# Second convolution as a six-stage pipeline in quarters of a chunk, with both parts of the spectral product summed on VectorE

## The chip, the cores and the metric

The kernel runs on one core of a Trainium2 chip. The metric is the device time of one execution in microseconds (us). Each kernel is run several times; the medians below come from runs in the fast state. A program on one core shows no die to compare with, so small differences are judged from several rounds and, inside the kernel, from the length of the changed stage in the profile.

In the profile the engines are PE (TensorE matmuls), PEld (TensorE weight loads), DVE (VectorE), ACT (ScalarE), POOL (GpSimd) and SP (SyncE, which issues the DMAs).

## The reference

A sequence of 2048 positions by 512 channels passes through four layers: convolution, attention, convolution, attention. The convolution, cut to what matters:

```python
def _A_ref(u, ...):                      # u: layernorm(x)
    K = ...                              # one real filter per channel, length L
    Kf = rfft(pad(K)); Uf = rfft(pad(u)) # along the sequence
    y = irfft(Uf * Kf)[:L]
    return y + u * Dskip
x = x + _A_ref(_layernorm(x), ...)       # first convolution
x = x + _B_ref(_layernorm(x), ...)       # attention in a sliding window
x = x + _A_ref(_layernorm(x), ...)       # second convolution: same filters
x = x + _B_ref(_layernorm(x), ...)
```

The kernel computes the transforms as matmuls. The filter spectra `Kt` are made during the first convolution and kept in memory, so the second one only loads them. It is the second convolution alone that the change rewrites.

## The kernel before

The 512 channels are four chunks of 128. Each chunk is worked in four quarters in the frequency part. The order in the second convolution is: forward transform of chunk dc+1, then products, inverse and final step of chunk dc.

```python
    def u_fft(self, dc, ln):
        dsl = slice(dc * DCH, (dc + 1) * DCH)
        U = self.one.tile([128, NJ, DCH], BF, name="U", tag="U")
        for j in range(NJ):                                   # 16 per chunk
            ln.norm(U[:, j, :], self.X[:, j, dsl], j)          # VectorE, 128 columns
        Z = self.s1(lambda j: U[:, j, :], DCH)                 # 32 matmuls, 4 copies by ScalarE
        xc = self.one.tile([128, 4, 2, 512], BF, name="xc", tag="xc", bufs=2)
        self.s2(Z, 4, [xc[:, c] for c in range(4)], "xc")      # per quarter: 8 transposes, zt on
        return xc                                              # VectorE, 4 matmuls, xc on ScalarE

    def finish(self, dc, xc, Kt, c0=0, c1=4):
        # ... (cut)
        def inverse(c, pa, pb):
            vp = self.pst([128, 2, 32, 2, 8])
            for g in range(4):
                sl = slice(g * 128, (g + 1) * 128)
                o = vp[:, g // 2, :, g % 2, :]
                nc.tensor.matmul(o, pa[:, 0, sl], IC[:, 0, :], start=True, stop=False)
                nc.tensor.matmul(o, pb[:, 1, sl], IC[:, 1, :], start=False, stop=False)
                nc.tensor.matmul(o, pb[:, 0, sl], IC[:, 2, :], start=False, stop=False)
                nc.tensor.matmul(o, pa[:, 1, sl], IC[:, 2, :], start=False, stop=True)
            # ... copy of vp to VT: first half by ScalarE, second half by VectorE
        pend = None
        for c in range(c0, c1 + 1):
            # ... (cut): pa and pb of this quarter
                nc.vector.tensor_tensor(pa[:], xc[:, c], Kt[:, c, 0:1, :].to_broadcast([128, 2, 512]), ALU.mult)
                nc.vector.tensor_tensor(pb[:], xc[:, c], Kt[:, c, 1:2, :].to_broadcast([128, 2, 512]), ALU.mult)
            # ... inverse of the quarter before
        # ... final: 32 + 4 matmuls a chunk, two copies to X by ScalarE

def a_layer(nc, tc, C, X, kt_dram, ln, ln_b):       # second convolution
        # ... (cut): pools (psA: 3 PSUM buffers), load of Kts, layernorm statistics
        xcs = {0: cv.u_fft(0, ln)}
        for dc in range(4):
            if dc < 3:
                xcs[dc + 1] = cv.u_fft(dc + 1, ln)
            cv.finish(dc, xcs.pop(dc), Kts[dc])
            if dc == 2:
                ln_b.gather(X, 0, 0, NJ)
        ln_b.gather(X, 1, 0, NJ)
        ln_b.finish(0, NJ)
```

The complex product is (xr + i xi)(Kr + i Ki). `pa` holds xr Kr and xi Kr, `pb` holds xr Ki and xi Ki. The sum xr Kr - xi Ki is not formed: the inverse lets TensorE add the parts in PSUM, which takes 16 matmuls of 256 columns a quarter. The order written here is not the order in which the engines run it: a scheduler in the framework orders the instructions of each engine.

Of the kernel before, what the change touches and what calls it, by code (L numbers as in the profile page):

```python
# [11 lines left out]
ALU = mybir.AluOpType  # L12
AX = mybir.AxisListType
F32 = mybir.dt.float32
BF = mybir.dt.bfloat16
# [4 lines left out]
D = 512  # L20
# [4 lines left out]
NJ = 16  # L25
# [3 lines left out]
DCH = 128  # L29
# [126 lines left out]
class Conv:  # L156
# [19 lines left out]
    def s1(self, rhs_j, n, drow=None):  # L176

        nc, F1 = self.nc, self.C["F1"]
        Z = self.z.tile([128, 2, 16, 128], BF, name="Z", tag="Z")
        for jq in range(NJ // 4):  # L180
            ps = self.pst([128, 2, 16, 32])
            for jj in range(4):
                j = jq * 4 + jj
                for r in range(2):
                    dk = drow is not None and j == 0 and r == 0
                    o = ps[:, r, 0:n // 8, jj * 8:(jj + 1) * 8]
                    nc.tensor.matmul(o, F1[:, j, r, :], rhs_j(j), start=True, stop=not dk)  # L187
                    if dk:
                        nc.tensor.matmul(o, self.C["onesr"][:], drow, start=False, stop=True)
            self.evac("z", Z[:, :, 0:n // 8, jq * 32:(jq + 1) * 32], ps[:, :, 0:n // 8, :])  # L190
        return Z

    def s2(self, Z, cs, dsts, what):

        nc, ident, C2 = self.nc, self.C["ident"], self.C["C2"]
        zts = {}

        def turn(i):
            pt = self.psT.tile([128, 2, 4, 128], BF, name="pt", tag="psT")
            for r in range(2):  # L200
                for g in range(4):
                    nc.tensor.transpose(pt[:, r, g, :], Z[:, r, i * 4 + g, :], ident[:])  # L202
            zt = self.w.tile([128, 2, 512], BF, name="zt", tag="zt")
            self.evac("zt_" + what, zt[:].rearrange("q r k -> q (r k)"), pt[:].rearrange("q r g k -> q (r g k)"))
            zts[i] = zt

        turn(0)
        for i in range(cs):
            if i + 1 < cs:
                turn(i + 1)  # L210
            zt = zts.pop(i)
            xp = self.pst([128, 2, 512])
            nc.tensor.matmul(xp[:, 0, :], C2[:, 0, :], zt[:, 0, :], start=True, stop=False)  # L213
            nc.tensor.matmul(xp[:, 0, :], C2[:, 2, :], zt[:, 1, :], start=False, stop=True)
            nc.tensor.matmul(xp[:, 1, :], C2[:, 1, :], zt[:, 0, :], start=True, stop=False)
            nc.tensor.matmul(xp[:, 1, :], C2[:, 0, :], zt[:, 1, :], start=False, stop=True)  # L216
            self.evac(what, dsts[i], xp[:])
# [329 lines left out]


def a_layer(nc, tc, C, X, kt_dram, ln, ln_b):
    with ExitStack() as es:  # L550
        kp = es.enter_context(tc.tile_pool(name="a_kt", bufs=4))
        psA = es.enter_context(tc.tile_pool(name="a_psA", bufs=3, space=PSUM))
        psT = es.enter_context(tc.tile_pool(name="a_psT", bufs=2, space=PSUM))
        Kts = []
        for dc in range(4):
            Kt = kp.tile([128, 4, 2, 512], BF, name="Kt", tag="Kt")
            nc.sync.dma_start(Kt[:], kt_dram[dc])
            Kts.append(Kt)
        cv = Conv(nc, tc, es, C, X, psA, psT, ("zt_xc", "vt1"), pbufs=3, vbufs=2)
        for j in range(0, NJ, 4):  # L560
            ln.gather(X, 0, j, j + 4)
        ln.finish(0, NJ)
        xcs = {0: cv.u_fft(0, ln)}
        for dc in range(4):
            if dc < 3:
                xcs[dc + 1] = cv.u_fft(dc + 1, ln)
            cv.finish(dc, xcs.pop(dc), Kts[dc])
            if dc == 2:
                ln_b.gather(X, 0, 0, NJ)
        ln_b.gather(X, 1, 0, NJ)  # L570
        ln_b.finish(0, NJ)
# [188 lines left out]
def kernel(  # L760
# [27 lines left out]
    Wt, Vp = load_b_weights(nc, tc, const2, B_wqkv, B_wo)  # L788
    b_layer(nc, tc, C, X, Wt, Vp, ln_b)
    a_layer(nc, tc, C, X, kt_dram, ln, ln_b)  # L790
    ov = out[0].rearrange("(p j) d -> p j d", j=NJ)
    b_layer(nc, tc, C, X, Wt, Vp, ln_b, lambda j0, j1: nc.sync.dma_start(ov[:, j0:j1, :], X[:, j0:j1, :]))
# [30 lines left out]
```

## Time and profile before

| | before |
|---|---|
| median of 4 runs | 663.84 us (660.38 to 664.5) |
| profiled run, span | 662.2 us |
| second convolution, from its first normalisation (418.33) to the first normalisation of the next layer (526.67) | 108.34 us |

Part 1 of the page of the kernel before gives busy time (share of the span) and number of instructions:

```profile
PE 467.0 (71%) x5880; PEld 306.2 (46%) x5913; DVE 516.4 (78%) x1001; ACT 325.2 (49%) x428; POOL 12.6 (2%) x49
```

These shares average over very different stages. The table of stretches for the second convolution (columns: stretch, its length, busy time of each engine with instruction count, granted TensorE clock, DMA share, GB/s), first for the whole stage, then for one inverse phase of it:

```profile
core 0: us, PE busy (x) PEld busy (x) DVE busy (x) ACT busy (x) POOL busy (x), PEclk, DMA share, GB/s
418.33:526.67 108.34, 81.13 (x716) 59.98 (x720) 67.06 (x181) 48.41 (x57) 0.00 (x0) 0.88 0.08 35
446.49:453.11 6.62, 5.84 (x51) 4.75 (x49) 6.62 (x11) 2.34 (x4) 0.00 (x0) 1.00 0.01 1
```

Over the stage no engine is full: PE 75%, DVE 62%, ACT 45%. In the inverse phase of the second line DVE is busy 6.62 of 6.62 us and PE 5.84. This stretch is VectorE's part of the phase. TensorE's own inverse matmuls start earlier, and from 444.59 to 451.57 us TensorE is busy 6.98 of 6.98 us: 64 matmuls 0.109 us apart, 1.75 us a quarter.

The view of waits for the same stage (who waited for whom, us in total, times, longest):

```profile
ACT VT L174 <- PE psA L244: 23.1, 16, 7.4
DVE zt L172 <- PE pt L202: 17.8, 10, 7.9
```

ScalarE waits 23.1 us for inverse matmuls and VectorE 17.8 us for transposes. The timeline of VectorE shows the phases (columns: start, duration, engine, line, operation, out<-in, shapes, count, and in brackets the idle time before and what ended it):

```profile
442.96 0.69 DVE L172 COPY zt<-pt 128x1024 bf16<-128x1024 bf16 x1 [1.40 <-PE pt L202]
446.49 0.69 DVE L257 TENSOR_TENSOR pb<-xc,Kt 128x1024 bf16<-128x1024 bf16 x1 [2.84 <-PE psA L244]
447.10 0.68 DVE L256 TENSOR_TENSOR pa<-xc,Kt 128x1024 bf16<-128x1024 bf16 x1
447.71 0.68 DVE L172 CAST VT<-psA 128x512 bf16<-128x512 f32 x1
448.31 0.68 DVE L257 TENSOR_TENSOR pb<-xc,Kt 128x1024 bf16<-128x1024 bf16 x1
...
453.11 0.68 DVE L172 CAST VT<-psA 128x512 bf16<-128x512 f32 x1
458.89 2.99 DVE L153 TENSOR_SCALAR U<-X,ln_rstd_a,ln_nb_a 128x128 bf16<-128x128 bf16 x13 [5.09 <-PE psA L187]
```

The first pb had to wait until an inverse matmul was done (2.84 us): the product tiles have three buffers, and the inverse matmuls read them. From 446.49 to 453.11 VectorE issues pb, pa, VT without a pause, 0.60 us from start to start. Then nothing for 5.09 us, until TensorE has freed the single U buffer. The next chunk's forward phase follows. The phases alternate with a period of some 24 us a chunk.

### The profile page before, as it was taken

Reading aid. Unit: us, or ns where it says so; the run is one execution under the profiler, and the core shown is the slowest. Engines: PE = TensorE matmul, PEld = TensorE weight load, DVE = VectorE, ACT = ScalarE, POOL = GpSimd, SP = SyncE. Lnnn points to the kernel's source line nnn. Section 1 sums busy time; section 2 is a strip of 40 time slices with the busy share of each in tenths; the row PEclk is TensorE's granted clock in tenths of the full one; section 3 lists DMA queues with packets and bytes.
Section 4 is the critical chain, followed back from the end, with each engine's and each line's share of the span. In section 5 each row is a group of like instructions: output and inputs, shape, how many; then the busy total and the mean of one; then the engine's idle time right before and its main releaser. Section 6 shows DMA issues by size and latency. Waiting matters only on the chain. (4 is left out here: it accounts for less than half of the span.)

```text
span 662.2 us, 13624 instructions
## 1 busy us (share of the span) xinstructions
PE 467.0 (71%) x5880; PEld 306.2 (46%) x5913; DVE 516.4 (78%) x1001; ACT 325.2 (49%) x428; POOL 12.6 (2%) x49
## 2 busy tenths in 40 slices
PE   1102837766767867679985899687986599876896
PEld 0001534554554555343334666455655453336763
DVE  5999899999999991368878997856538659778960
ACT  5990434655555646346672134564453265753133
POOL 0000000000000002000000000000000000000000
PEclk9999977998897889779997999779989799986999
DMA  9000100200200203200003000600000000030011
GB/s 303 24 0 1 34 16 18 96 8 29 97 12 24 97 19 112 96 0 1 1 17 94 2 1 2 253 1 1 1 1 1 0 1 1 1 109 2 2 65 64
DMA packets 14794, 26.70 MB, mean 40 GB/s; under 512 B 4753, under 2 KB 10258, under 8 KB 13582
## 3 DMA queue, kind: packets, MB, share of 16 engines
q1 hardware_dynamic: 12334, 24.65, 10.5%
q10 hardware_dynamic: 2400, 1.18, 0.7%
q8 instruction: 46, 0.75, 0.5%
q14 instruction: 14, 0.11, 0.1%
HBM read 13.80 MB, written 8.39 MB: 34 GB/s over the span
## 5 line engine op out<-in xcount | busy, mean ns | idle before, releaser
L613 PE MATMUL ps_qk<-xnT,wqk 128*128 128x512 bf16 x246 | 61.2, 380 | 1.6 <-ACT kT_4692 L615 0.3
L187 PE MATMUL psA<-U,sb_F_128 128*128 128x128 bf16 x256 | 24.1, 241 | 47.0 <-issue 38.5
L174 ACT CAST Z<-psA 128x1024 bf16<-128x1024 f32 (+1 forms) x52 | 46.4, 962 | 20.7 <-issue 17.8
L174 ACT CAST xc<-psA 128x1024 bf16<-128x1024 f32 x32 | 32.0, 1012 | 46.5 <-PE psA L216 39.9
L187 PEld LDWEIGHTS <-sb_F_128 128*128 128x128 bf16 x416 | 27.0, 104 | 57.6 <-issue 51.3
L202 PE MATMUL pt<-sb_ident,Z 128*128 128x128 bf16 x384 | 37.9, 265 | 19.1 <-ACT Z L174 19.1
L174 ACT CAST VT<-psA 128x512 bf16<-128x512 f32 x48 | 26.5, 587 | 43.3 <-PE psA L244 43.3
L202 PEld LDWEIGHTS <-Z 128*128 128x128 bf16 x384 | 32.5, 122 | 31.2 <-ACT Z L174 21.5
L731 ACT CAST oT<-po 128x1024 bf16<-128x1024 f32 x16 | 15.4, 1015 | 58.7 <-PE po L728 58.7
L241 PE MATMUL psA<-sb_IC,pa 128*128 128x256 bf16 x128 | 35.9, 280 | 7.9 <-DVE pa L256 7.8
L172 DVE COPY zt<-pt 128x1024 bf16<-128x1024 bf16 x32 | 21.8, 690 | 23.4 <-PE pt L202 23.2
L153 DVE TENSOR_SCALAR U<-X,ln_rstd_a,ln_nb_a 128x128 bf16<-128x128 bf16 x128 | 33.9, 313 | 7.2 <-PE psA L187 7.1
L242 PE MATMUL psA<-sb_IC,pb 128*128 128x256 bf16 x128 | 36.1, 282 | 1.6 <-DVE pb L257 1.3
L613 PEld LDWEIGHTS <-wqk 128*128 128x128 bf16 x256 | 22.8, 98 | 29.5 <-issue 8.2
L737 PE MATMUL ps_o<-wo_t,oT 128*128 128x512 bf16 x122 | 33.6, 379 | 3.9 <-ACT oT L731 3.1
L244 PE MATMUL psA<-sb_IC,pa 128*128 128x256 bf16 x128 | 36.1, 282 | 0.0
L243 PE MATMUL psA<-sb_IC,pb 128*128 128x256 bf16 x128 | 36.1, 282 | 0.0
L461 PE MATMUL psk<-Ytab,Xtab 128*32 128x64 bf16 x1024 | 23.4, 207 | 12.9 <-DVE Ytab L445 7.0
L464 PE MATMUL psk<-Y2tab,Xtab 128*32 128x48 bf16 x1024 | 22.6, 203 | 13.3 <-issue 11.4
L655 PE MATMUL Lp<-prod,sb_bones 128*32 128x512 bf16 x256 | 24.7, 392 | 10.3 <-DVE prod L650 7.5
L213 PE MATMUL psA<-zt,sb_C_120 128*128 128x512 bf16 x48 | 22.7, 473 | 11.2 <-DVE zt L172 6.0
L140 DVE BATCH_NORM_STATS2 ln_st_b<-X 128x6 f32<-128x384 bf16 (+1 forms) x64 | 21.3, 413 | 11.4 <-ACT X L272 11.4
(402 smaller groups left out, 1211.1 us busy)
## 6 DMA issues: line engine op xcount, KB each, us to landing
Kt<-kt_scratch SPq DMA_DIRECT2D x4, 1024.0 KB, 7.0
Vp<-V SPq DMA_DIRECT2D x2, 1568.0 KB, 9.2
kt_scratch<-Kt SPq DMA_DIRECT2D x3, 1024.0 KB, 3.8
X<-in_A_u_dram SPq DMA_DIRECT2D x4, 512.0 KB, 5.5
k_scratch<-KTq SPq DMA_DIRECT2D x8, 256.0 KB, 2.4
KT<-k_scratch SPq DMA_DIRECT2D x8, 256.0 KB, 2.7
out_dram<-X SPq DMA_DIRECT2D x4, 512.0 KB, 2.6
sb_F_128<-c_F SPq DMA_DIRECT2D x1, 1024.0 KB, 5.9
```

The costliest lines, as they stand in the source:

```text
L153: self.nc.vector.tensor_scalar(dst, src, self.rstd[:, j:j + 1], self.nb[:, j:j + 1], ALU.mult, ALU.add)
L174: self.nc.scalar.copy(dst, src)
L187: nc.tensor.matmul(o, F1[:, j, r, :], rhs_j(j), start=True, stop=not dk)
L202: nc.tensor.transpose(pt[:, r, g, :], Z[:, r, i * 4 + g, :], ident[:])
L241: nc.tensor.matmul(o, pa[:, 0, sl], IC[:, 0, :], start=True, stop=False)
L242: nc.tensor.matmul(o, pb[:, 1, sl], IC[:, 1, :], start=False, stop=False)
L243: nc.tensor.matmul(o, pb[:, 0, sl], IC[:, 2, :], start=False, stop=False)
L244: nc.tensor.matmul(o, pa[:, 1, sl], IC[:, 2, :], start=False, stop=True)
L461: nc.tensor.matmul(psk[32 * g:32 * g + 32, ds, :], xs, Y[:, m // 2, h, :, t], start=(m == 0), stop=False, skip_group_check=True)
L613: nc.tensor.matmul(ps[:], wqk[:, ct, f0:f0 + 128], xnT[:, ct, s0:s0 + 512], start=(ct == 0), stop=(ct == 3))
L655: nc.tensor.matmul(Lp[r0:r0 + 32, w // 4, :], bones[:, w % 4, :], pr[:, f2, hb * 512:(hb + 1) * 512], start=(w % 4 == 0), stop=(w % 4 == 3 ...
L737: nc.tensor.matmul(ps[:], oT[:, ft, j * 128:(j + 1) * 128], wo_t[:, ft, :], start=(ft == 0), stop=False)
```

## The change

The intent is to keep all engines at work on different quarters at once. The stages of 16 quarters are issued with fixed lags, so that in one step the loop handles the forward matmuls of quarter k, the transposes of k-5, the second transform of k-6, the product of k-7, the inverse of k-8 and the final step of k-13. At the same time VectorE forms the complex sum `Y`, so the inverse needs 8 matmuls a quarter, not 16. The normalisation becomes 16 instructions of 512 columns ahead of the pipeline.

```diff
 def a_layer(nc, tc, C, X, kt_dram, ln, ln_b):
     with ExitStack() as es:
+        # ... pools: U whole, Z 3 buffers, xc 4, VT 2, work tiles 3
         psA = es.enter_context(tc.tile_pool(name="a_psA", bufs=3, space=PSUM))
         psT = es.enter_context(tc.tile_pool(name="a_psT", bufs=2, space=PSUM))
+        def s1(k):      # ... 8 matmuls, Z on ScalarE
+        def turn(k):    # ... 8 transposes, zt on VectorE
+        def s2(k):      # ... 4 matmuls, xc on ScalarE
+        def product(k):
+            # ...
+            nc.vector.tensor_tensor(pa[:], x[:], Kt[dc][:, c, 0:1, :].to_broadcast([128, 2, 512]), ALU.mult)
+            nc.vector.tensor_tensor(pb[:], x[:], Kt[dc][:, c, 1:2, :].to_broadcast([128, 2, 512]), ALU.mult)
+            nc.vector.tensor_tensor(Y[k][:, 0, :], pa[:, 0, :], pb[:, 1, :], ALU.subtract)
+            nc.vector.tensor_tensor(Y[k][:, 1, :], pa[:, 1, :], pb[:, 0, :], ALU.add)
+        def inverse(k):
+            # ...
+            for g in range(4):
+                nc.tensor.matmul(o, y[:, 0, sl], IC[:, 0, :], start=True, stop=False)
+                nc.tensor.matmul(o, y[:, 1, sl], IC[:, 2, :], start=False, stop=True)
+            # ... VT: half gh == 0 by ScalarE, half gh == 1 by VectorE, as before
+        def final(k):   # ... 1 + 8 matmuls, one copy to X by ScalarE
         # ... statistics, as before
-        xcs = {0: cv.u_fft(0, ln)}
-        for dc in range(4):
-            # ... (cut)
+        for j in range(NJ):
+            ln.norm(U[:, j, :], X[:, j, :], j)
+        for k in range(16 + 14):
+            for fn, lag in ((final, 13), (inverse, 8), (product, 7), (s2, 6), (turn, 5), (s1, 0)):
+                if 0 <= k - lag < 16:
+                    fn(k - lag)
+            if k == 13 + 11:
                 ln_b.gather(X, 0, 0, NJ)
         ln_b.gather(X, 1, 0, NJ)
         ln_b.finish(0, NJ)
```

More of the change, by code (lines that the diff above doesn't have):

```diff
@@ L550, in a_layer @@
     with ExitStack() as es:
+        big = es.enter_context(tc.tile_pool(name="a_big", bufs=1))
         kp = es.enter_context(tc.tile_pool(name="a_kt", bufs=4))
+        zp = es.enter_context(tc.tile_pool(name="a_z", bufs=3))
+        cp = es.enter_context(tc.tile_pool(name="a_xc", bufs=4))
+        vpool = es.enter_context(tc.tile_pool(name="a_vt", bufs=2))
+        wk = es.enter_context(tc.tile_pool(name="a_wk", bufs=3))
         psA = es.enter_context(tc.tile_pool(name="a_psA", bufs=3, space=PSUM))
@@ L553, in a_layer @@
         psT = es.enter_context(tc.tile_pool(name="a_psT", bufs=2, space=PSUM))
-        Kts = []
+        ident, C2, IC, F1, F1T = C["ident"], C["C2"], C["IC"], C["F1"], C["F1T"]
+        U = big.tile([128, NJ, D], BF, name="U")
+        Kt = []
         for dc in range(4):
-            Kt = kp.tile([128, 4, 2, 512], BF, name="Kt", tag="Kt")
-            nc.sync.dma_start(Kt[:], kt_dram[dc])
-            Kts.append(Kt)
-        cv = Conv(nc, tc, es, C, X, psA, psT, ("zt_xc", "vt1"), pbufs=3, vbufs=2)
+            t = kp.tile([128, 4, 2, 512], BF, name="Kt", tag="Kt")
+            nc.sync.dma_start(t[:], kt_dram[dc])
+            Kt.append(t)
@@ new lines, in a_layer @@
+        Z, zt, xc, Y, VT = {}, {}, {}, {}, {}
+        def s1(k):
+            dc, q = k // 4, k % 4
+            if q == 0:
+                Z[dc] = zp.tile([128, 2, 16, 128], BF, name="Z", tag="Z")
+            ps = psA.tile([128, 2, 16, 32], F32, name="ps_s1", tag="psA")
+            for jj in range(4):
+                j = q * 4 + jj
+                for r in range(2):
+                    nc.tensor.matmul(ps[:, r, :, jj * 8:(jj + 1) * 8], F1[:, j, r, :],
+                                     U[:, j, dc * DCH:(dc + 1) * DCH], start=True, stop=True)
+            nc.scalar.copy(Z[dc][:, :, :, q * 32:(q + 1) * 32], ps[:])
@@ new lines, in turn @@
+        def turn(k):
+            dc, c = k // 4, k % 4
+            pt = psT.tile([128, 2, 4, 128], BF, name="pt", tag="psT")
+            for r in range(2):
+                for g in range(4):
+                    nc.tensor.transpose(pt[:, r, g, :], Z[dc][:, r, c * 4 + g, :], ident[:])
+            zt[k] = wk.tile([128, 2, 512], BF, name="zt", tag="zt")
+            nc.vector.tensor_copy(zt[k][:].rearrange("q r k -> q (r k)"), pt[:].rearrange("q r g k -> q (r g k)"))
+        def s2(k):
+            z = zt.pop(k)
+            xp = psA.tile([128, 2, 512], F32, name="xp", tag="psA")
+            nc.tensor.matmul(xp[:, 0, :], C2[:, 0, :], z[:, 0, :], start=True, stop=False)
+            nc.tensor.matmul(xp[:, 0, :], C2[:, 2, :], z[:, 1, :], start=False, stop=True)
+            nc.tensor.matmul(xp[:, 1, :], C2[:, 1, :], z[:, 0, :], start=True, stop=False)
+            nc.tensor.matmul(xp[:, 1, :], C2[:, 0, :], z[:, 1, :], start=False, stop=True)
+            xc[k] = cp.tile([128, 2, 512], BF, name="xc", tag="xc")
+            nc.scalar.copy(xc[k][:], xp[:])
@@ new lines, in product @@
+        def product(k):
+            dc, c = k // 4, k % 4
+            x = xc.pop(k)
+            pa = wk.tile([128, 2, 512], BF, name="pa", tag="pa")
+            pb = wk.tile([128, 2, 512], BF, name="pb", tag="pb")
+            Y[k] = wk.tile([128, 2, 512], BF, name="Y", tag="Y")
+            nc.vector.tensor_tensor(pa[:], x[:], Kt[dc][:, c, 0:1, :].to_broadcast([128, 2, 512]), ALU.mult)
+            nc.vector.tensor_tensor(pb[:], x[:], Kt[dc][:, c, 1:2, :].to_broadcast([128, 2, 512]), ALU.mult)
+            nc.vector.tensor_tensor(Y[k][:, 0, :], pa[:, 0, :], pb[:, 1, :], ALU.subtract)
+            nc.vector.tensor_tensor(Y[k][:, 1, :], pa[:, 1, :], pb[:, 0, :], ALU.add)
@@ new lines, in inverse @@
+        def inverse(k):
+            dc, c = k // 4, k % 4
+            if c == 0:
+                VT[dc] = vpool.tile([128, 2, NJ, DCH], BF, name="VT", tag="VT")
+            y = Y.pop(k)
+            vp = psA.tile([128, 2, 32, 2, 8], F32, name="vp", tag="psA")
+            for g in range(4):
+                sl = slice(g * 128, (g + 1) * 128)
+                o = vp[:, g // 2, :, g % 2, :]
+                nc.tensor.matmul(o, y[:, 0, sl], IC[:, 0, :], start=True, stop=False)
+                nc.tensor.matmul(o, y[:, 1, sl], IC[:, 2, :], start=False, stop=True)
+            for gh in range(2):
+                x0 = c * 32 + gh * 16
+                dst = VT[dc][:, :, :, x0:x0 + 16].rearrange("k r j x -> k (r j) x")
+                src = vp[:, gh, :, :, :].rearrange("k rj g e -> k rj (g e)")
+                if gh == 0:
+                    nc.scalar.copy(dst, src)
+                else:
+                    nc.vector.tensor_copy(dst, src)
@@ new lines, in final @@
+        def final(k):
+            dc, q = k // 4, k % 4
+            dsl = slice(dc * DCH, (dc + 1) * DCH)
+            ps = psA.tile([128, 4, DCH], F32, name="ps_y", tag="psA")
+            j0 = q * 4
+            nc.tensor.matmul(ps[:], ident[:], X[:, j0:j0 + 4, dsl], start=True, stop=False, skip_group_check=True)
+            for jj in range(4):
+                for r in range(2):
+                    nc.tensor.matmul(ps[:, jj, :], F1T[:, j0 + jj, r, :], VT[dc][:, r, j0 + jj, :],
+                                     start=False, stop=(jj == 3 and r == 1), skip_group_check=True)
+            nc.scalar.copy(X[:, j0:j0 + 4, dsl], ps[:])
@@ L562, in a_layer @@
         ln.finish(0, NJ)
-        xcs = {0: cv.u_fft(0, ln)}
-        for dc in range(4):
-            if dc < 3:
-                xcs[dc + 1] = cv.u_fft(dc + 1, ln)
-            cv.finish(dc, xcs.pop(dc), Kts[dc])
-            if dc == 2:
+        for j in range(NJ):
[5 more added lines that the diff above has]
+            if k == 13 + 11:
                 ln_b.gather(X, 0, 0, NJ)
```

## The prediction

> **What bounds the kernel now.** The change touches only the second convolution. In the timeline it runs from the end of the statistics before it (418.3 us) to the first normalisation of the layer after it (526.7 us): 108.4 of 662.2 us. Within 425 to 526.2 us the table of stretches shows PE busy 76.5, DVE 60.4, ACT 44.7 of 101 us: nothing is full. The timeline shows why: four chunks go through phases in turn, each bound by another engine. Forward: copies of Z (ACT, 0.94 us pitch), then transposes, zt, matmuls, xc (DVE waits 17.8 us for transposes in the view of waits). Inverse: PE alone, 16 matmuls, 1.75 us a quarter, while ACT waits 23.1 us.
>
> **What changes, per quarter (16 of them), by pitches in the timeline.**
> - PE: inverse from 16 to 8 matmuls, 1.73 to 0.87 us at full clock. With forward 0.45, transposes 0.45, s2 0.86, final 0.67: 3.3 us.
> - DVE: adds a subtract and an add of 128x512 bf16. pa (128x1024) has 0.60 us pitch; half of it plus fixed cost gives an estimate of 0.33 each, and 0.1 for waits on its own products. The Trainium skill, "VectorE: DVE Perf Modes", section Mode 2×_1P, says packed 16-bit operands give two results a cycle; the 0.60 us agrees. With zt, pa, pb, VT at 0.60 each: 3.1 to 3.2 us.
> - ACT: Z 0.94, xc 0.97, VT 0.55, X 0.55: 3.0 us, nearly unchanged.
> - DVE normalisation: 64 instructions of 128 columns (0.23 each, 15 us) become 16 of 512 (0.37 each, 6 us), all ahead of the pipeline. This pays for most of the 10.6 us of adds.
>
> So DVE's work stays at 66 to 70 us and becomes, with PE, the limit. The gain comes from overlap and 14 us less PE work.
>
> **On the critical path.** Fill: norm until 424.3, last Z copy of chunk 0 about 425.5, first Y about 431. Then 15 quarters. The engines are balanced at 3.0 to 3.3 us and coupled: three PSUM buffers serve four tiles a quarter, and the final matmuls wait for the DVE copy of VT, which waits for the ACT copy. I estimate 3.6 us a quarter: last Y about 485. Drain: the scheduled DVE order puts the statistics of chunks 0 to 2 (16 x 0.47) after the last products, so about 13 us (7.5 + 0.6 + 3.2 + 1.3 + 0.9) lie between the last Y and the first normalisation: 498. The stage falls from 108 to about 80 us, saving 27 to 28. The other layers keep their times.
>
> **Clock.** "TensorE: Matmul & The Clock Gate", Part 1, says the array runs at half rate after an idle window. The trace agrees: s2 matmuls come 0.43 us apart near 426 and 487, 0.215 elsewhere. A pipeline leaves no such gaps except at its start, so I expect at least the present clock of 0.89.
>
> **Prediction: 637 us** (8 in 10: 627 to 648). Faster by over 2%: 0.94; within 2%: 0.05; slower: 0.01.
>
> **Right if** the stage takes 75 to 85 us; DVE and PE are busy 80% or more in its middle; successive pa come 3.3 to 3.9 us apart; Y subtract and add take 0.35 to 0.45 us; after the last VT copy DVE runs statistics back to back for some 10 us. **Wrong if** a quarter takes over 4.2 us, through the chain inverse, VT on ACT, VT on DVE, Y in one in-order queue, or late PSUM buffers, or half-clock spells; or if the layer after runs at another clock.

## The result and the profile after

| | before | after |
|---|---|---|
| median of 4 runs | 663.84 us | 630.23 us (627.81 to 631.95) |
| profiled run, span | 662.2 us | 630.0 us |
| second convolution | 108.34 us | 73.55 us (420.89 to 494.44) |

The ratio is 0.9501, with a 95% interval from 0.9449 to 0.9553. A ratio is the mean time of one kernel's fast runs over that of the other's of the same rounds, so it is not quite the ratio of the medians quoted. The stage became 34.8 us shorter and the span 32.2 us: the part ahead of the stage, whose code is the same, took 2.6 us more in this profile. Its end lies between 416.4 and 420.9 us in all profiles, in no order that follows the edits. So lengths of the stage are the sharper measure below. From the end of the stage to the end of the span it is 135.6 us after and 135.5 before.

Part 1 of the page of the kernel after:

```profile
PE 449.9 (71%) x5748; PEld 293.6 (47%) x5785; DVE 517.8 (82%) x985; ACT 326.2 (52%) x436; POOL 12.6 (2%) x49
```

VectorE's 517.8 us are the 516.4 of before within 0.3%, while TensorE has lost 17 us. The table of stretches, for the stage and for three parts of its middle (from the first pa to the last one; columns as in the table before):

```profile
420.89:494.44 73.55, 59.14 (x584) 43.75 (x592) 67.85 (x164) 49.30 (x65) 0.00 (x0) 0.92 0.12 50
432.46:450.30 17.84, 15.91 (x170) 11.73 (x171) 17.84 (x36) 14.62 (x18) 0.00 (x0) 1.00 0.01 1
450.30:463.28 12.98, 12.75 (x138) 9.96 (x138) 12.83 (x25) 11.66 (x16) 0.00 (x0) 1.00 0.01 3
463.28:478.42 15.14, 14.58 (x136) 10.27 (x137) 15.04 (x30) 10.95 (x16) 0.00 (x0) 1.00 0.00 1
```

VectorE is busy 99% of the middle (17.84 of 17.84, 12.83 of 12.98, 15.04 of 15.14 us), TensorE 89 to 98%, at a granted clock of 1.00. The view of waits answers to that of before:

```profile
ACT VT L627 <- PE vp L621: 6.3, 12, 0.9
...
DVE zt L588 <- PE pt L586: 3.4, 1, 3.4
```

ScalarE's wait for inverse matmuls fell from 23.1 to 6.3 us, and VectorE's wait for transposes from 17.8 to 3.4 us, all of it one wait in the start. VectorE's timeline, one early quarter and the start of a late one:

```profile
444.16 0.68 DVE L606 TENSOR_TENSOR pa<-xc,Kt 128x1024 bf16<-128x1024 bf16 x1
444.76 0.68 DVE L607 TENSOR_TENSOR pb<-xc,Kt 128x1024 bf16<-128x1024 bf16 x1
445.36 0.69 DVE L588 COPY zt<-pt 128x1024 bf16<-128x1024 bf16 x1
445.96 0.68 DVE L629 CAST VT<-vp 128x512 bf16<-128x512 f32 x1
446.56 0.42 DVE L608 TENSOR_TENSOR Y<-pa,pb 128x512 bf16<-128x512 bf16 x1
446.89 0.42 DVE L609 TENSOR_TENSOR Y<-pa,pb 128x512 bf16<-128x512 bf16 x1
447.23 0.69 DVE L606 TENSOR_TENSOR pa<-xc,Kt 128x1024 bf16<-128x1024 bf16 x1
...
460.06 0.68 DVE L606 TENSOR_TENSOR pa<-xc,Kt 128x1024 bf16<-128x1024 bf16 x1
460.66 0.68 DVE L607 TENSOR_TENSOR pb<-xc,Kt 128x1024 bf16<-128x1024 bf16 x1
461.38 0.42 DVE L608 TENSOR_TENSOR Y<-pa,pb 128x512 bf16<-128x512 bf16 x1
```

From pa to pa it is 3.07 us, and this is the plain sum of the starts: pa, pb, zt, VT at 0.60 each and Y twice at 0.33. No bracket: the view shows no wait of VectorE for another engine here. In the late quarter the subtract follows pb directly and starts 0.72 us after it, not 0.60: it needs pb's result, and no other instruction fills the 0.12 us. That gives 3.2 us a quarter. Two quarters took longer without a bracket, 3.15 us from 450.30 and 3.41 us from 453.45. In the second VectorE started VT and the next pa 0.07 and 0.13 us late; this pa followed the end of its xc copy on ScalarE by 0.04 us. The inputs come close before their use throughout: each xc copy ended 0.03 to 0.76 us before the pa that reads it. The end of the stage:

```profile
481.02 0.42 DVE L609 TENSOR_TENSOR Y<-pa,pb 128x512 bf16<-128x512 bf16 x1
481.36 1.93 DVE L140 BATCH_NORM_STATS2 ln_st_b<-X 128x6 f32<-128x384 bf16 x4
483.20 0.68 DVE L629 CAST VT<-vp 128x512 bf16<-128x512 f32 x1
483.81 8.24 DVE L140 BATCH_NORM_STATS2 ln_st_b<-X 128x6 f32<-128x384 bf16 x27
491.96 1.27 DVE L145 BATCH_NORM_AGGREGATE ln_mv_b<-ln_st_b 128x2 f32<-128x12 f32 x16
...
494.44 1.71 DVE L153 TENSOR_SCALAR xn<-X,ln_rstd_b,ln_nb_b 128x512 bf16<-128x512 bf16 x5
```

After the last add (481.02 + 0.42) VectorE works almost without pause for 13.0 us: 31 statistics and one VT copy, the aggregation, then small steps to the first normalisation of the next layer.

### The profile page after: what moved, and what is told of

Its sections match the earlier page's. It is cut to its first block, busy times and chain, and to the rows that moved or that the text cites. A ratio compares the mean times of both kernels' runs of the same rounds, so it can differ in the third digit from the quotient of the medians.

```text
span 630.0 us, 13342 instructions
## 1 busy us (share of the span) xinstructions
PE 449.9 (71%) x5748; PEld 293.6 (47%) x5785; DVE 517.8 (82%) x985; ACT 326.2 (52%) x436; POOL 12.6 (2%) x49
## 4 chain that ended last, share of the span: by engine, by line
PE 29%; DVE 23%; issue 7%; ACT 5%; DMA 1%; POOL 0%; ACTq 0%; POOLq 0%; DVEq 0%
PE ps_qk L697 8%; PE ps_v L707 4%; PE ps_o L821 4%; PE po L812 2%; DVE ln_st_b L140 2%; PE Lp L739 2%; DVE pa L606 1%; DVE pb L607 1%; DVE VT L629 1%; DVE zt L588 1%; DVE prod L734 1%; PE ps_o L823 1%; DVE xn L153 1%; DMA wo_t<-in_B_wo_dram 1%; ACT oT L815 1%
## 5 line engine op out<-in xcount | busy, mean ns | idle before, releaser
L187 PE MATMUL psA<-U,sb_F_128 128*128 128x128 bf16 x128 | 13.6, 249 | 41.8 <-issue 38.5
L174 ACT CAST Z<-psA 128x1024 bf16<-128x1024 f32 (+1 forms) x36 | 31.3, 928 | 18.4 <-issue 17.5
L202 PE MATMUL pt<-sb_ident,Z 128*128 128x128 bf16 x256 | 28.5, 287 | 11.8 <-ACT Z L174 11.8
L174 ACT CAST xc<-psA 128x1024 bf16<-128x1024 f32 x16 | 15.9, 1012 | 27.3 <-PE psA L216 27.3
L461 PEld LDWEIGHTS <-Xtab 128*32 128x32 bf16 x1024 | 20.7, 105 | 18.5 <-issue 17.6
L445 DVE TENSOR_TENSOR Ytab<-Ytab,MA 128x2048 bf16<-128x2048 bf16 x24 | 29.2, 1219 | 0.1
L447 DVE TENSOR_TENSOR Y2tab<-Ytab,MB 128x2048 bf16<-128x2048 bf16 x24 | 29.2, 1218 | 0.0
L707 PE MATMUL ps_v<-wv,xnT 128*128 128x512 bf16 x126 | 28.2, 379 | 0.1
L140 DVE BATCH_NORM_STATS2 ln_st_a<-X 128x6 f32<-128x512 bf16 x32 | 21.0, 686 | 7.1 <-ACT X L824 5.3
L824 ACT CAST X<-ps_o 128x512 bf16<-128x512 f32 x32 | 18.3, 586 | 16.0 <-PE ps_o L823 16.0
```

What stands on the lines that cost most here:

```text
L140: self.nc.vector.bn_stats(self.st[:, j, part, :], X[:, j, a:b])
L174: self.nc.scalar.copy(dst, src)
L187: nc.tensor.matmul(o, F1[:, j, r, :], rhs_j(j), start=True, stop=not dk)
L202: nc.tensor.transpose(pt[:, r, g, :], Z[:, r, i * 4 + g, :], ident[:])
L445: nc.vector.tensor_tensor(Y[:, :, :, q * EYB:(q + 1) * EYB, :].rearrange("n c h e t -> n (c h) e t"), src, self.mult(self.MA, lev, hc, EYB ...
L447: nc.vector.tensor_tensor(Y2[:, :, :, (q - 1) * EYB:q * EYB, :].rearrange("n c h e t -> n (c h) e t"), src, self.mult(self.MB, lev, hc, EY ...
```

## The experiments

The two marked kernels leave out part of the product, so their result is not the convolution. The check calls every run correct, these two as well; it therefore doesn't show that the sum of this layer is right. "Stage" is the time from the first normalisation of the second convolution to the first one of the next layer, read in the timeline of the profiled run; "pace" is the distance of successive pa.

| run | what | median us | ratio to before | stage us |
|---|---|---|---|---|
| e0_after_again | the changed kernel | 630.01 | 0.9494 | 73.54 |
| e1_pipe_only | pipeline, no sum, 16 inverse matmuls | 634.88 | 0.958 | 79.52 |
| e2_sum_only | old order, sum, 8 inverse matmuls | 652.85 | 0.984 | 95.93 |
| e9_old_no_sum | old order, 8 inverse matmuls, no sum (wrong result) | 648.49 | 0.9778 | 93.13 |
| e3_sum_twice | changed, sum done twice | 640.00 | 0.9649 | 83.78 |
| e4_no_sum | changed, no sum (wrong result) | 624.23 | 0.9411 | 68.15 |
| e5_norm_chunks | changed, normalisation by chunks | 633.72 | 0.9552 | 78.50 |
| e8_psum2 | changed, two PSUM buffers | 635.89 | 0.958 | 78.83 |
| e6_vt_late_act | changed, late VT on ScalarE | 625.68 | 0.9435 | 70.53 |
| e7_best | e6 plus two further moves | 626.31 | 0.9445 | 70.79 |

e1 to e4 share one chip and one set of runs of the kernel before (median 662.37), e0 and e5 to e7 another (663.91), e8 and e9 a third (663.26). e0, e5, e6 and e7 had five rounds, the others three.

The theory to test: the pipeline turns a chain of phases into one stage paced by its fullest engine, VectorE, at the sum of its instruction starts. The rivals: the gain is the saved TensorE work; or the pace is set by coupling, the loop from the inverse through the two VT copies, or the PSUM buffers, and VectorE only looks full.

### The changed kernel again

No edit. 

> The changed kernel itself, as the reference on this chip: 0.950 of the kernel before, 628 to 632 us; the stage 73.5 us again.

It measured as expected: 630.01 us and a stage of 73.54 us, 0.01 us from the first profile.

### The pipeline without the sum

```diff
-            nc.vector.tensor_tensor(Y[k][:, 0, :], pa[:, 0, :], pb[:, 1, :], ALU.subtract)
-            nc.vector.tensor_tensor(Y[k][:, 1, :], pa[:, 1, :], pb[:, 0, :], ALU.add)
+            Y[k] = (pa, pb)
 # and in inverse(k), the four matmuls of before:
-                nc.tensor.matmul(o, y[:, 0, sl], IC[:, 0, :], start=True, stop=False)
-                nc.tensor.matmul(o, y[:, 1, sl], IC[:, 2, :], start=False, stop=True)
+                nc.tensor.matmul(o, pa[:, 0, sl], IC[:, 0, :], start=True, stop=False)
+                nc.tensor.matmul(o, pb[:, 1, sl], IC[:, 1, :], start=False, stop=False)
+                nc.tensor.matmul(o, pb[:, 0, sl], IC[:, 2, :], start=False, stop=False)
+                nc.tensor.matmul(o, pa[:, 1, sl], IC[:, 2, :], start=False, stop=True)
```

> The pipeline without the sum on VectorE: products pa and pb go to the inverse unsummed, 16 matmuls a quarter again. Theory (the pipeline brings most of the gain and whichever engine has the most work per quarter sets the pace): VectorE needs about 2.45 us a quarter, TensorE about 3.5 (no final matmuls yet), 4.2 (all parts) and 3.7 (no forward part any more), so TensorE sets a pace of about 3.7 us against the 3.1 us of the changed kernel; the stage takes 80 to 86 us against 73.6, the whole 637 to 643 us, with TensorE busy over 95% and VectorE about 65% in the middle. Rival (the saved inverse matmuls bring the gain): 650 us or more.

It measured 634.88 us and a stage of 79.52 us, 0.5 us below the expected range; the whole was 2 us below its range. The pace was 3.50, 4.17 and 3.72 us in the three parts, which are the sums of TensorE's work. The table of stretches of this run, four quarters with all parts and then four without a forward part:

```profile
448.54:465.20 16.66, 16.55 (x180) 13.57 (x180) 10.50 (x17) 11.97 (x16) 0.00 (x0) 1.00 0.00 1
465.20:480.08 14.88, 14.77 (x148) 11.80 (x149) 10.50 (x18) 8.73 (x12) 0.00 (x0) 1.00 0.01 2
```

TensorE is busy 16.55 of 16.66 us and VectorE 10.50. The limit changed engines, as the theory said. The pipeline without the sum brings 28.8 of the 34.8 us of the stage. This run still holds everything but the sum: the lags, the added buffers and the normalisation in 16 instructions. A rival stays untested: no run gave the old order the added buffers, though its normalisation waited 6.2 us in all for the single U buffer, so what the lags bring by themselves is not shown.

### The sum in the old order

```diff
+        self.summed = summed        # True only for the second convolution
 # in inverse:
+                if self.summed:
+                    nc.tensor.matmul(o, pa[:, 0, sl], IC[:, 0, :], start=True, stop=False)
+                    nc.tensor.matmul(o, pa[:, 1, sl], IC[:, 2, :], start=False, stop=True)
+                    continue
 # after pa and pb:
+                if self.summed:
+                    Y = self.p.tile([128, 2, 512], BF, name="Y", tag="Y")
+                    nc.vector.tensor_tensor(Y[:, 0, :], pa[:, 0, :], pb[:, 1, :], ALU.subtract)
+                    nc.vector.tensor_tensor(Y[:, 1, :], pa[:, 1, :], pb[:, 0, :], ALU.add)
+                    pa = Y
```

> The old order of phases with the sum on VectorE in the second convolution only. Theory: the inverse phase, which TensorE bounded at 1.75 us a quarter, becomes a VectorE phase of about 2.5 us (pa, pb, VT at 0.6 and the two halves of Y at 0.33), so taking 14 us of work off TensorE gains nothing; 660 to 675 us. Rival (TensorE work was the limit of the old kernel, so halving the inverse pays by itself): 648 to 653 us.

My theory missed: 652.85 us, within the rival's range, and a stage 12.4 us shorter. In the timeline of VectorE in this run the products stand elsewhere:

```profile
462.01 0.69 DVE L173 COPY zt<-pt 128x1024 bf16<-128x1024 bf16 x1 [1.29 <-PE pt L203]
462.62 0.68 DVE L261 TENSOR_TENSOR pa<-xc,Kt 128x1024 bf16<-128x1024 bf16 x1
463.21 0.68 DVE L262 TENSOR_TENSOR pb<-xc,Kt 128x1024 bf16<-128x1024 bf16 x1
464.04 0.69 DVE L173 COPY zt<-pt 128x1024 bf16<-128x1024 bf16 x1
464.65 0.68 DVE L261 TENSOR_TENSOR pa<-xc,Kt 128x1024 bf16<-128x1024 bf16 x1
465.24 0.68 DVE L262 TENSOR_TENSOR pb<-xc,Kt 128x1024 bf16<-128x1024 bf16 x1
466.73 0.42 DVE L265 TENSOR_TENSOR Y<-pa,pb 128x512 bf16<-128x512 bf16 x1 [0.80 <-PE psA L244]
```

The products of two quarters sit between the zt copies of the next chunk's forward phase. In the kernel before, 13 of the 16 pairs of products came once an inverse phase had begun, since its matmuls held the product buffers (VectorE waited for them 2.84, 2.77 and 2.77 us). Here only the adds read pa and pb, so these are free again early; what waits for an inverse matmul now is the subtract (0.80 us), whose Y tile has three buffers of its own. So the idle time of the forward phase took part of the work. I had counted VectorE's work of the inverse phase as bound to that phase.

### The old order with the short inverse and no sum

This is the edit of the run before without the two lines that form Y; the inverse reads pa alone, so the result is wrong.

> Wrong result on purpose: the old order of phases, eight inverse matmuls, no subtract and add. It splits the 10 us that the sum alone gained in the old order. Theory, formed after that run: TensorE was on the path of the inverse phase, so halving it pays nearly its full 14 us, and the adds cost some 2 to 5 us of the 10.6 they take, since VectorE waits elsewhere: 646 to 650 us. Rival: the adds cost nothing there: 652 us. Second rival: they cost their full 10.6 us: 641 us.

It measured 648.49 us, within the expected range, and a stage of 93.13 us. So in the old order the shorter inverse gave 15.2 us of the stage, and the adds took back 2.8 us of it, though VectorE was busy 10.0 us longer with them (77.59 against 67.57 us): most of that fell into idle time. The timeline of VectorE also shows which products moved:

```profile
460.64 0.69 DVE L262 TENSOR_TENSOR pb<-xc,Kt 128x1024 bf16<-128x1024 bf16 x1
461.31 0.69 DVE L173 COPY zt<-pt 128x1024 bf16<-128x1024 bf16 x1
461.92 0.68 DVE L262 TENSOR_TENSOR pb<-xc,Kt 128x1024 bf16<-128x1024 bf16 x1
...
464.01 0.69 DVE L261 TENSOR_TENSOR pa<-xc,Kt 128x1024 bf16<-128x1024 bf16 x1
```

Only pb, which nothing reads in this run, comes between the zt copies; pa, which the inverse reads, still comes after the first inverse matmul (462.94 us), though VectorE stood idle for 0.62 us before the third pb, which came at 463.22 us. With the inverse equally short in both runs, this points to the buffers, and not to the shorter inverse, as what let the products move. One thing stays open: the 15.2 us mix two effects, less TensorE work (128 matmuls at 0.109 us are 14 us) and products that get a buffer earlier. No run held the order fixed.

### The sum twice

```diff
+            for _ in range(2):
+                nc.vector.tensor_tensor(Y[k][:, 0, :], pa[:, 0, :], pb[:, 1, :], ALU.subtract)
+                nc.vector.tensor_tensor(Y[k][:, 1, :], pa[:, 1, :], pb[:, 0, :], ALU.add)
```

> The changed kernel with the subtract and the add done twice (same result). Theory (VectorE is the only limit of the pipeline): 16 times 0.66 us = 10.6 us more in full, 640 to 642 us against about 630.5. Rival (the pace is set by the loop inverse, VT copies, buffers of PSUM, and VectorE only looks full): less than 4 us more.

It measured 640.00 us and a stage 10.2 us longer, a pace of 3.74 us against 3.07. The full cost of 0.67 us a quarter shows. An engine that only looked full would have hidden part of it. The rival of coupling (less than 4 us more) falls. A loop that runs through VectorE's adds would also have grown by their cost; against it stands the timeline of the changed kernel, where VectorE's starts follow one another at 0.60 and 0.33 us, almost without a gap.

### No sum in the pipeline

The inverse reads pa alone and the two lines that form Y are gone; the result is wrong.

> Wrong result on purpose: the changed kernel without the subtract and the add, the inverse reads pa alone. Theory: VectorE falls to 2.45 us a quarter and the next limit is TensorE at about 2.65 us early and 2.85 us late (at full clock), so only about 5 to 6 us of the 10.6 come back: 624 to 626 us, TensorE busy over 95% in the middle. Rival (coupling, loop): within 2 us of the changed kernel. Rival (VectorE remains the limit): 10 us less, 620 us.

It measured 624.23 us, and the stage fell by 5.4 us, half of the adds' 10.7 us. The table of stretches, first all parts, then no forward part:

```profile
446.42:459.59 13.17, 13.06 (x148) 10.44 (x148) 10.50 (x18) 11.85 (x16) 0.00 (x0) 1.00 0.01 2
459.59:470.97 11.38, 11.28 (x116) 8.66 (x117) 10.50 (x17) 8.74 (x12) 0.00 (x0) 1.00 0.01 2
```

The pace is 3.29 and 2.85 us with TensorE busy 13.06 of 13.17 and 11.28 of 11.38 us. So TensorE is the next limit, close behind VectorE. The paces of the pipeline without the sum lie 0.88 and 0.87 us higher (4.17 and 3.72), which is eight more matmuls at 0.109 us: TensorE paces both runs. In the few quarters that have all parts TensorE is even the higher of the two (3.29 against 3.07 to 3.2); the changed kernel's one quarter of 3.41 us falls among these.

### The normalisation by chunks

```diff
-        for j in range(NJ):
-            ln.norm(U[:, j, :], X[:, j, :], j)
 # in s1(k), at the first quarter of a chunk:
+                for j in range(NJ):
+                    dsl = slice(dc * DCH, (dc + 1) * DCH)
+                    ln.norm(U[:, j, dsl], X[:, j, dsl], j)
```

> The changed kernel with the normalisation put back to 64 instructions of 128 columns, chunk by chunk, inside the pipeline. Theory (VectorE sets the pace from the first product on): 64 x 0.23 = 14.7 us instead of 5.3 is 9.4 us more VectorE work, of which about 2 to 3 us fall into the start, where VectorE waits; 6 to 8 us more than the changed kernel, 636 to 639 us. Rival (one instruction or many, it is hidden behind TensorE and ScalarE): within 2 us.

It measured 633.72 us, 3.7 us more than the changed kernel, with a stage 5.0 us longer: the direction of the theory, below its range. VectorE was busy 76.59 us in the stage against 67.84, 8.7 us more, but its idle time fell from 5.7 to 1.9 us. In the start VectorE waits while TensorE and ScalarE fill the pipeline. Up to the first pa its idle time fell from 5.0 us (6.55 busy of 11.57) to none (9.98 of 10.00), more than the 2 to 3 I had assumed, and the first pa came 1.6 us sooner; some 1.2 us of new idle time in the middle took part of that back.

### Two PSUM buffers

```diff
-        psA = es.enter_context(tc.tile_pool(name="a_psA", bufs=3, space=PSUM))
+        psA = es.enter_context(tc.tile_pool(name="a_psA", bufs=2, space=PSUM))
```

> The changed kernel with two PSUM buffers of the shared kind instead of three. The four tiles of a quarter each hold a buffer for about 1.4 to 2.4 us (matmuls, waits, copies), 6.9 to 7.5 us in all. Theory (three buffers, 2.3 to 2.5 us a quarter, were enough below the 3.1 us of VectorE): two give 3.5 us or more and become the limit, 636 us or more, and VectorE waits in the middle. Rival (PSUM buffers play no part): within 2 us.

It measured 635.89 us, 0.1 us below the expected range, with a stage 5.3 us longer. The expected 3.5 us or more came in four quarters only. The pace went to 4.14 to 4.27 us in the four quarters where most kinds of tile are alive at once, and stayed at 3.41 us or below in the others. The view of waits in those four quarters:

```profile
DVE VT L629 <- ACT VT L627: 2.3, 3, 0.9
...
PE ps_s L577 <- DVE VT L629: 1.1, 2, 0.5
PE vp L620 <- ACT Z L579: 0.9, 3, 0.4
```

The forward matmuls wait for VectorE's VT copy and the inverse for ScalarE's Z copy: these read the buffers that the matmuls want to write. VectorE in turn waits for the VT copy of ScalarE. With three buffers the view shows none of these waits for VectorE in the middle. So the coupling that I feared is real with two buffers and costs almost nothing with three.

### The late VT copies on ScalarE

VectorE is the limit and ScalarE has room once it no longer copies Z. The Trainium skill, "Perfetto Trace Analysis", section Optimizing Scalar/DVE Operations, says that moving work to ScalarE may make sense when VectorE is saturated.

```diff
-                if gh == 0:
+                if gh == 0 or k >= 8:
                     nc.scalar.copy(dst, src)
```

> The changed kernel with both halves of VT copied by ScalarE for the last 8 quarters, where ScalarE no longer copies Z. VectorE has 0.6 us less there (2.6 us), ScalarE 2.6 us, TensorE 2.85 us at full clock. Theory (VectorE sets the pace, TensorE is the next limit): the pace of these quarters goes from 3.2 to 2.85 us, with the last copy some 3 us less in all: about 627 us. Rival (the pace is set by the loop from the inverse through the VT copies): no change or slower, as the two halves are copied one after the other anyway.

It measured 625.68 us and a stage of 70.53 us, 3.0 us less than the changed kernel; the pace of the late quarters went from 3.2 to 2.85 us, which is TensorE's number in the run without the sum. No kernel with the full sum was faster: ratio 0.9435 (0.9406 to 0.9465) against 0.9494 (0.9462 to 0.9527) for the changed kernel in the same rounds. The next run can't be told from it.

### Two more moves

```diff
-                if gh == 0:
+                if gh == 0 or k >= 8 or k in (0, 2, 4):
 # and the normalisation of chunk 0 first:
-            ln.norm(U[:, j, :], X[:, j, :], j)
+            ln.norm(U[:, j, 0:DCH], X[:, j, 0:DCH], j)
+        for j in range(NJ):
+            ln.norm(U[:, j, DCH:D], X[:, j, DCH:D], j)
```

> As the run before, and ScalarE also copies both halves of VT in quarters 0, 2 and 4, and the columns of chunk 0 are normalised first (16 x 128 columns), the other 384 after them, so that the first matmuls get their input sooner. Theory: start 1 to 1.5 us shorter, early pace from 3.07 to about 2.9 us on average: 1 to 2.5 us less than the run before, 624 to 626 us. If the start is set by TensorE at half clock or by the copies of Z, only the early pace gains: 626 us.

It brought nothing: 626.31 us and a stage of 70.79 us. The first pa came 0.5 us sooner after the start (11.07 against 11.57 us), where 1 to 1.5 us had been expected. But the first five quarters took 15.43 us against 14.76 in the run before it. In the first of them VectorE waited 0.89 us for transposes, which I did not trace further; the pa that opens the third waited 0.58 us for an xc copy that stood behind both VT copies in ScalarE's queue.

## Why the prediction was right

The sum of the prediction had three terms, and each can be set beside the trace.

| term | predicted | measured |
|---|---|---|
| start to first Y | about 12.7 us (431 - 418.3) | 13.4 us (434.27 - 420.89) |
| 15 quarters, from the first Y to the last | 15 x 3.6 = 54 us | 45.8 us (434.27 to 480.10), 15 x 3.06 |
| the last Y itself, with a VT copy inside | not counted | 1.3 us |
| last Y to the first normalisation | about 13 us | 13.0 us |
| stage | about 80 us | 73.55 us |
| whole kernel | 637 us (627 to 648) | 630.23 us |

- **The mechanism was right.** The stage fell by overlap, with VectorE's work unchanged (67.06 us busy before, 67.85 after) and as the limit, TensorE close behind. The runs with the sum done twice (+10.2 us) and left out (-5.4 us) show both limits. Two of the five signs under "Right if" still failed: the stage took 73.55 us, not 75 to 85, and of the distances of successive pa only one (3.41 us) lay in 3.3 to 3.9 us. So the total owes something to luck: 630.23 us lies near the lower end of a range of 21 us, and two smaller errors, below, made up for part of the large one.
- **The term that was mis-sized is the pace**: "I estimate 3.6 us a quarter". I had the engines' sums right (VectorE 3.1 to 3.2 us; the trace shows 3.07 and 3.2) and then added about 0.5 us for coupling, through three PSUM buffers and the chain of VT copies. Almost none showed: beyond the 0.12 us after pb, which the prediction had counted as 0.1, the quarters lost some 0.3 us in all (the one of 3.15 and the one of 3.41 us). The reserve behind this is small: the xc copies ended 0.03 to 0.76 us before the pa that read them, and with two buffers the waits appear. This term is about 8 us too high, more than the 6.8 us of the whole: the start took 0.7 us more than predicted, and 1.3 us of the last Y itself were in no term. In the start the last Z copy of chunk 0 ended 8.0 us after the first normalisation, not 7.2 us: in the trace TensorE works on matmuls of chunk 1 between those of chunk 0's last quarter.
- **"This pays for most of the 10.6 us of adds"**: the normalisation saved VectorE 8.7 us of busy time, and 5.0 us of the stage; the rest would have gone into its idle time.
- **"The gain comes from overlap and 14 us less PE work"** holds, but the two don't add. The pipeline without the sum takes 28.8 us off the stage, the sum alone 12.4, both 34.8. Once the pipeline is there the sum trades TensorE's 3.50 to 4.17 us a quarter for VectorE's 3.07 to 3.2, worth 6.0 us.
- **"Inverse: PE alone"** was half right. TensorE ran that phase without a break, but VectorE needed 1.80 us a quarter there, as much as TensorE's 1.75 (6.62 of 6.62 us busy in the table of stretches), partly with products for the next quarters. It did not hurt the total, but a like blind spot, work bound to its phase, made my expectation of the sum alone wrong.
- **The clock** of the stage went from 0.88 to 0.92, and was 1.00 through the middle, as expected. The start of the stage ran at 0.70 (420.89 to 432.46 us). So did that of the kernel before (0.71 over its first 11.57 us), from which the prediction took its times, so the clock does not explain the longer start.

The Trainium skill, "Perfetto Trace Analysis", section Optimization Strategy, says that kernels with several regimes, each with another most-contended engine, may gain from interleaving them. This case agrees: with VectorE's work the same, interleaving took the stage from 62% to 92% VectorE busy and from 108.3 to 73.6 us.

## What to carry to other kernels

When each phase of a loop fills another engine, add up the work of each engine over one unit of the loop. The pipeline of this case, with three PSUM buffers, ran within some 0.3 us in all of VectorE's sum, the largest in most quarters, plus a start and an end that can be read off the schedule; with two buffers it did not. Taking work from the fullest engine was then worth the distance to the next sum, not the work itself (5.4 us of 10.7). Before calling moved work hidden or exposed, check in the order of instructions where it lands, and who holds the buffers that it writes.

## What the Trainium skill lacked or had wrong

- "Perfetto Trace Analysis", section Optimizing Scalar/DVE Operations, gives VectorE about 60 ns of fixed cost an instruction on SBUF and about 125 ns on PSUM. Here a 128x1024 bf16 product from SBUF and a 128x512 fp32 copy from PSUM both start 0.60 us apart, and 128x512 products 0.33 us apart. Two sizes of product give 0.52 ns a column and an estimate of about 67 ns fixed. The 128x1024 bf16 copy zt, which reads PSUM, also takes 0.60 us from start to start, as much as the product of that size from SBUF. If the 128x512 fp32 copy takes one element a cycle at 0.96 GHz (the clock in "VectorE: DVE Perf Modes", section Specifications), an estimate for it is 67 ns as well, not 125.
- None of the pages read gives a figure for the cost of a VectorE instruction that reads the result of the one right before it. Here it is 0.12 us: the subtract starts 0.72 us after pb where it follows it directly. Where copies stand between, every start is 0.60 us after the one before, and nothing is lost. In the changed kernel this is the step from 3.07 to 3.2 us a quarter.
- "ScalarE: Activation LUTs", section What ACT_TABLE_LOAD costs, gives about 1283 ns for the load, which the trace shows to the nanosecond (1283 ns), and 1380 ns more for a drain. In the trace of the changed kernel the load starts at 418.69 us, right after the copy before it, and the next activation starts at 420.08 us, so no such drain is seen there.
